# More difference steps in the early blocks, and an earlier pair of sums in block 22

## The chip, the cores and the metric

The kernel runs on one core of a Trainium2 chip. The metric is device time in microseconds for one execution. The kernel before takes 592.43 us in the median of three runs (592.17 to 593.26). "PE" is the matrix engine TensorE, "PEld" its weight loads, "DVE" VectorE, "ACT" ScalarE, "POOL" GpSimd, and "SP" the engine that issues the stores.

## What is computed

The input x has 8 batches of 3008 rows and 256 columns. The reference takes the real part of the two-dimensional Fourier transform of each batch, multiplies the 24064 resulting rows by a 256 x 2048 matrix, takes the squared positive part, and multiplies by a 2048 x 256 matrix:

```python
X = np.fft.fft(x, axis=1)
X = np.fft.fft(X, axis=2)
x = X.real.reshape(B * S, D)
h = np.maximum(x @ w_in, 0.0)
return (h * h @ w_out).astype(np.float32)
```

## The kernel before

**Blocks and their two halves.** The output rows come in pairs: from the same cosine part and sine part of a transformed row (tiles `zc` and `zs`) follow the row k, as P+Q, and its mirror image, as P-Q. P is the product of the weights with `zc`, Q that with `zs`. So the kernel works on 12040 columns instead of 24064 rows. They are cut into 25 blocks (`wins`, w = 0 to 24); block 0 has 240 columns, block 1 has 512, blocks 2 and 3 have 376 each, block 4 has 512, block 5 has 448, the others 512 and the last one 360. Each block fills a tile `h2` of 16 chunks of the 2048 hidden features, with the P+Q results in half 0 (columns 0 to wn) and the P-Q results in half 1, and the block after it multiplies that `h2` by the second weight matrix (`ffn2_steps`, L713 to L757).

**Steps.** A block has eight steps s, two chunks of 128 features each. There are two kinds of steps (loop from L1054):

- A plain step: `pq` (L917) puts P+Q into a PSUM bank with four matmuls; ScalarE rectifies it into half 0 (`first`, `relu`, L966 and L946); `turn` (L941) adds -2Q with two more matmuls; ScalarE rectifies P-Q into half 1. The squares of both halves are done by VectorE as one operation (`power`, L958), which `keep` (L955) puts on a list that `settle` (L843) empties in the following step.
- A difference step, one of those listed in `diff`: `cosines` (L926) puts only P into the bank. VectorE computes t2 = -2P + N from it (`twice`, L932). Two matmuls add Q (`sines`, L936), and may do so only when `twice` has read the bank. ScalarE rectifies P+Q, and VectorE gets the other half as the saturated sum of t2 and the bank (the custom operation at L951). No `turn` is needed, so PE runs four matmuls and not six. N is the Nyquist row that the turned weights would have contributed; it comes in a tile `n2` per step. Half 0 is squared by ScalarE (`power_act`, L962, over the list `plus`), half 1 by VectorE, alone or with another step's.

**N rows.** `spread_nyq` (L851) stores one row of `zs` to DRAM from ScalarE's queue (`rd`) and loads it back to 128 partitions from GpSimd's queue (`zn`). `nyq_rows` (L858) then makes `n2` from it, two GpSimd operations per step; three such tiles exist. `nyq` (L984) calls them in the block before, from step `hi` on, and for what is left in step 0.

**Between the matmuls of a step** `others` (L971) issues what else is due: a share of the block before's second layer (a quarter of its 256 columns per job; jobs 0 to 7 are the groups 0 and 1 of 128 columns, then each group has four jobs, one per quarter of the 16 chunks), jobs of the transform (`at`), and, in steps `lo` to `hi` - 1, the matmuls that make `zc` and `zs` of the next block (`z_steps`, L538). Each of these two parts ends with a copy on ScalarE (L570) for the first columns and with `apart` (L585, VectorE L588) for the rest, called "the sums" here. If the next step is a difference step (`held["on"]`), the sums wait in `held["jobs"]` and are issued by `let_go` at the end of the next `settle`, so behind that step's `twice` and squares.

**Order.** All engines issue in the order in which the program names the instructions. The order is written by hand: `pend` holds the second rectifier of a difference step until after the next `twice` if the next step is a difference step too; `aside` holds squares until the next plain step, where they go behind its `pq`; `aside_act` holds squares for ScalarE, issued by `act_squares` at the end of a step. In blocks 3 and 4 the squares of step 6 go as one through `aside` (`twin`). Blocks 21, 23 and 24, and block 22 from step 6 on, have a third PSUM bank for steps (`px`).

**Where difference steps stand before.** Blocks 0 to 2 have none; blocks 3, 4 and 5 have steps 4 and 6; block 22 has 1, 2, 4, 5, 6, 7 and block 23 has 1, 2, 3, 5, 6, 7.

Of the kernel before, what the change touches and what calls it, by code (L numbers as in the profile page):

```python
# [29 lines left out]
def kernel(  # L30
# [49 lines left out]
    NW = len(wins)  # L80
# [687 lines left out]
    NST = NFC // 2  # L768
# [3 lines left out]
    diff[NW - 4] = diff[NW - 2] = (1, 2, 3, 5, 6, 7)  # L772
    diff[NW - 1] = (1, 2, 3, 4, 5, 6, 7)
    diff[NW - 3] = (1, 2, 4, 5, 6, 7)
    threes = (NW - 4, NW - 2, NW - 1)
    pairs = []
    by_act = (2, 5)
# [3 lines left out]
    def put(w, s, i, name, *k, d=at_of):  # L781
        d[w][s].append(lambda: folds[i][name](*k))
# [7 lines left out]
    for i in range(2, B):  # L790
        b0 = (win_of(col_of[i, 0]) + win_of(col_of[i - 1, 1])) // 2 - 1
        tight = b0 - 2 in [(win_of(col_of[j, 0]) + win_of(col_of[j - 1, 1])) // 2 - 1 for j in range(2, i)]
        near = i == 2 or tight
        at_of[b0 - 1][0].append(lambda i=i: make(i))
        calm = not near and not need[b0]
        at_of[b0 - 2][5 if calm else 7].append(lambda i=i: load_rows(i))
        backs.append(b0)
        late(b0 + 1, 3, i, 0)
        late(b0 + 1, 4, i, 1)
        for k in (2, 3, 4):  # L800
            late(b0 + 1, 5, i, k)
        put(b0 - 1, 4 if tight else 3 if i == 2 else 5 if near else 1 if calm else 3, i, "d_rows")
        put(b0 - 1, 5 if near else 3, i, "d_even", 0)
        put(b0 - 1, (6 if tight else 7) if near else 5, i, "d_even", 1)
        put(b0 if i == 2 else b0 - 1, 0 if i == 2 else 7, i, "n_cos")
        put(b0, 0, i, "d_odd", 0)
        put(b0, 1, i, "d_odd", 1)
        put(b0, 2, i, "n_sin")
        put(b0, 3, i, "even")
        put(b0, 4, i, "away")  # L810
        put(b0, 5, i, "odds")
        put(b0, 6, i, "back")
        put(b0, 6, i, "nyq", d=post_of)
        if i + 1 < B and (win_of(col_of[i + 1, 0]) + win_of(col_of[i, 1])) // 2 - 1 > b0 + 2:
            put(b0 + 1, 2, i, "load")
        else:
            put(b0, 7, i, "load")
        if b0 > 5:
            diff[b0] = (2, 4, 6, 7) if tight else (2, 4, 6)
            diff[b0 + 1] = (1, 2, 4, 6, 7)  # L820
            shared.append(b0 + 1)
        if calm:
            diff[b0 - 1] = (1, 2, 4, 6, 7)
            shared.append(b0 - 1)
            pairs.append(b0 - 1)
        if tight:
            diff[b0 - 1] = (1, 2, 4)
            shared.remove(b0 - 1)
# [5 lines left out]
    third = []  # L834
    aside = []
    aside_act = []

    def act_squares():
        run(*aside_act)
# [3 lines left out]
    def settle():  # L843
        for k in kept:
            k()
        kept.clear()
        let_go()
# [19 lines left out]
    for w in range(NW):  # L867
# [16 lines left out]
        if w == 1:  # L884
            fj = fold_jobs(1)
            at = [[], fj[0:1], fj[1:2], fj[2:3], fj[3:5], [], [], []]
            post[5] = fj[5:6]
        elif w == 2:
            te = table_steps(1)
            at = [[folds[1]["even"], folds[1]["away"]], [lambda: te["freq"](), lambda: te["args"](0)], [lambda: f0s["v_part"](0)], [lambda: f0s["v_part"](1), f0s["even"], f0s["away"], f0s["back"]],  # L890
                  [lambda: te["turns"](0)], [lambda: te["mods"](0)], [lambda: te["absm"](0), lambda: te["sins"](0)], [lambda: te["coss"](0)]]
        elif w == 3:
            at[0] = [lambda: te["weigh"]()]
            for st in range(5):
                at[1 + st // 3] = at[1 + st // 3] + f0s["late"][st : st + 1]
            at[3] = [folds[1]["back"]]
            lo, hi = 3, NST - 1
        elif w == win_of(col_of[1, 1]) - 1:
            for st in range(5):
                at[min(st, 3)] += folds[1]["late"][st : st + 1]  # L900
            lo, hi = 4, NST - 1
# [53 lines left out]
        def keep(*k):  # L955
            kept.append(lambda p=power: p(*k))
# [61 lines left out]
        if w == 0:  # L1018
            run(lambda: quad(0), lambda: quad_relu(0, 0), lambda: quad(1), lambda: quad_relu(1, 0))
            run(lambda: gh_step(2, False), lambda: gh_turn(2))  # L1020
            run(lambda: quad_turn(0), lambda: quad_relu(0, 1), lambda: quad_turn(1), lambda: quad_relu(1, 1))
            run(lambda: gh_step(3, False), lambda: gh_turn(3))
            run(lambda: quad(2), lambda: quad_relu(2, 0), lambda: quad(3), lambda: quad_relu(3, 0), *rm[1::2])
            run(lambda: quad_turn(2), lambda: quad_relu(2, 1), lambda: quad_turn(3), lambda: quad_relu(3, 1), *(lambda p=p: quad_power(p) for p in range(4)))
        elif w == 1:
            zl = [j for zu, part, h in zj for j in zu(part, h)]
            for p in range(NST // 2):
                s0, s1 = 2 * p, 2 * p + 1
                f2q = spread(f2, p, NST // 2)
                n = len(f2q) // 4  # L1030
                pq(s0)
                if p < 2:
                    settle()
                relu(s0, 0)
                pq(s1)
                relu(s1, 0)
                if s1 == NST - 1:
                    run(*post[s0 - 1])
                    settle()
                    power(s1, 0, 1)  # L1040
                    run(*zl)
                run(*f2q[0:n])
                turn(s0)
                run(*f2q[n : 2 * n])
                turn(s1)
                relu(s0, 1)
                relu(s1, 1)
                run(*at[s0], *at[s1], *f2q[2 * n :])
                if p == 2:
                    kept.pop(0)()  # L1050
                keep(s0, 0, 2)
                keep(s1, int(s1 == NST - 1), 2)
            gh_nyq()
        for s in range(NST) if w > 1 else ():  # L1054
            held["on"] = s + 1 in diff.get(w, ())
            if w == NW - 3 and s == 6:
                more_banks()
            if s in diff.get(w, ()):
                cosines(s)
                twice(s)  # L1060
                if w in pairs and s == 4:
                    kept.extend(aside)
                    aside.clear()
                run(*pend)
                pend.clear()
                settle()
                if made[s + 1]:
                    run(*plus)
                    plus.clear()
                others(s)  # L1070
                sines(s)
                first(s)
                twin = w < 5 and s == 6
                whole = twin or w in shared and s == 4 or w in threes[:2] or w in pairs or w == NW - 3 or w == NW - 1 and s in by_act
                pend.append(lambda s=s, r=relu, k=keep, whole=whole: (r(s, 1), whole or k(s, 1, 2)))
                if w in threes[:2] and s % 4 == 1 or w in pairs and s in (1, 6) or w == NW - 3 and s in (1, 4):
                    aside.append(lambda s=s, p=power: p(s, 1, 2, 2))
                if not made[s + 3]:
                    run(*pend)
                    pend.clear()  # L1080
                if twin:
                    aside.append(lambda s=s, p=power: p(s, 0, 2))
                else:
                    plus.append(lambda s=s, p=power_act: p(s))
                act_squares()
                if w == NW - 3 and s == 6:
                    aside.append(lambda s=s, p=power: p(s, 1, 2))
                if w in threes[:2] and s % 4 == 3 or w == NW - 3 and s == 7 or w == NW - 1 and s in by_act:
                    aside_act.append(lambda s=s, p=power_act: p(s, 1))
                nyq(s)  # L1090
                continue
            if made[s] and made[s + 1] and w not in threes and w not in pairs:
                f2s[s].pop(0)()
            pq(s)
            if not (w in pairs and s == 3):
                kept.extend(aside)
                aside.clear()
            settle()
            first(s)
            if s == NST - 1:  # L1100
                power(s, 0, 1)
            others(s)
            nyq(s)
            turn(s)
            relu(s, 1)
            act_squares()
            if w in shared and s == 5:
                power_act(4, 1)
            keep(s, int(s == NST - 1), 2)
        settle()  # L1110
        old = (w, h2)
    run(*plus)
# [33 lines left out]
```

## Time and profile before

| what | value |
|---|---|
| median of 3 runs | 592.43 us (592.17 to 593.26) |
| the profiled execution | 592.23 us |
| its span | 590.5 us |
| granted TensorE clock, mean | 0.999 |
| blocks 2 and 3 | 48.36 to 69.97 and 69.97 to 88.63 us |
| block 5 | 110.18 to 132.53 us |
| blocks 22 and 23 | 510.02 to 534.16 and 534.16 to 556.43 us |

The span is the time between the first and the last profiled instruction; 1.7 us of the execution lie around it. A row of a timeline reads: start, duration, engine, line of the kernel, operation, what it writes and from what, shape, count, and in square brackets how long the engine stood idle before it and what ended that. Consecutive instructions of one kind are one row. The starts of matmuls are as recorded, their ends are modelled and lie in the next matmul, so durations of matmuls are read from start to start.

### The profile page before, as it was taken

To read this page: it belongs to the slowest core of one execution; us is meant where nothing else is said; L and a number is where in the kernel's file an instruction comes from. 1 tells how busy PE (TensorE), PEld (TensorE's weight loads), DVE (VectorE), ACT (ScalarE), POOL (GpSimd) and SP (SyncE) were. 2 spreads that over 40 slices of the span, in tenths; PEclk is the share of its full clock that TensorE was granted. 3 is DMA by queue.
4 is the path that set the end of the run, shared out by engine and by line. 5 is a ranking of instruction groups with operands and counts; after the bars stand their busy time and mean duration, and the time that the engine had idled before them with its cause. 6 is when DMAs were issued, how large, how long until landed. Compare 5 with 4: busy or idle time off the path is not lost. (4 is left out here: it accounts for less than half of the span.)

```text
span 590.5 us, 11333 instructions
## 1 busy us (share of the span) xinstructions
PE 580.8 (98%) x4408; PEld 424.2 (72%) x4408; DVE 503.5 (85%) x579; ACT 474.2 (80%) x630; POOL 266.2 (45%) x325
## 2 busy tenths in 40 slices
PE   8999999999999999999999999999999999999997
PEld 4567786776777777767777777777777777776786
DVE  7988687987889787988999799979899798888881
ACT  7796878867887787788888798878888788988982
POOL 8520423267324626382454651555605825437230
PEclk9999999999999999999999999999999999999999
DMA  8945421133612561237124441146312311211222
GB/s 150 179 88 128 125 73 44 55 101 72 136 48 55 132 137 55 70 92 163 42 58 118 93 116 52 39 122 122 84 40 89 99 48 41 60 47 47 61 57 71
DMA packets 37625, 50.33 MB, mean 85 GB/s; under 512 B 4589, under 2 KB 30755, under 8 KB 37571
## 3 DMA queue, kind: packets, MB, share of 16 engines
q0 software_dynamic: 10400, 24.94, 21.0%
q1 hardware_dynamic: 26899, 24.44, 13.7%
q8 instruction: 34, 0.56, 0.4%
q10 hardware_dynamic: 272, 0.23, 0.1%
q14 instruction: 20, 0.16, 0.1%
HBM read 36.42 MB, written 27.86 MB: 109 GB/s over the span
## 5 line engine op out<-in xcount | busy, mean ns | idle before, releaser
L730 PE MATMUL po<-wout,h 128*128 128x256 f16 (+1 forms) x3024 | 364.4, 273 | 0.0
L730 PEld LDWEIGHTS <-h 128*128 128x128 f16 (+1 forms) x3024 | 296.8, 98 | 74.8
L953 ACT ACTIVATE h<-ph 128x1024 f16<-128x1024 f32 (+3 forms) x264 | 252.6, 989 | 58.1 <-PE ph L939 38.0
L864 POOL TENSOR_SCALAR n<-zn,g2n 128x512 f32<-128x512 f16 (+3 forms) x188 | 177.1, 956 | 79.9 <-DMA zn<-rd 56.9
L960 DVE TENSOR_TENSOR h<-h 128x2048 f16<-128x2048 f16 (+5 forms) x175 | 175.1, 1009 | 18.1 <-ACT h L953 15.4
L934 DVE SCALAR_TENSOR_TENSOR t<-ph,n 128x1024 f32<-128x1024 f32 (+3 forms) x84 | 100.3, 1194 | 30.7 <-PE ph L930 21.9
L964 ACT ACTIVATE h<-h 128x1024 f16<-128x1024 f16 (+3 forms) x107 | 110.3, 1033 | 1.5 <-DVE zs L588 0.4
L951 DVE CUSTOM_DVE_ANT_0 h<-t,ph 128x1024 f16<-128x1024 f32 x75 | 91.1, 1215 | 12.0 <-ACT h L953 11.5
L856 POOL DMA_DIRECT2D zn<-rd x22 | 12.8, 582 | 139.9 <-DMA rd<-zs 126.0
L745 ACT ACTIVATE osb<-po 128x512 f32<-128x512 f32 (+3 forms) x95 | 54.9, 582 | 24.4 <-PE po L730 19.8
L921 PE MATMUL ph<-zc,gh 128*128 128x512 f16 (+2 forms) x180 | 66.1, 368 | 0.4 <-ACT h L1012 0.3
L922 PE MATMUL ph<-zs,gh 128*128 128x512 f16 (+2 forms) x180 | 66.1, 368 | 0.0
L944 PE MATMUL ph<-zs,gh 128*128 128x512 f16 (+2 forms) x180 | 51.4, 367 | 0.0
L939 PE MATMUL ph<-zs,gh 128*128 128x512 f16 (+3 forms) x168 | 49.0, 373 | 1.6 <-DVE t L934 1.1
L930 PE MATMUL ph<-zc,gh 128*128 128x512 f16 (+3 forms) x168 | 49.0, 373 | 0.0
L930 PEld LDWEIGHTS <-gh 128*128 128x128 f16 x188 | 18.4, 98 | 21.0
L921 PEld LDWEIGHTS <-gh 128*128 128x128 f16 x196 | 19.1, 97 | 20.0 <-DVE h L951 0.7
L922 PEld LDWEIGHTS <-gh 128*128 128x128 f16 x196 | 19.1, 98 | 19.8 <-issue 0.7
L953 ACT ACTIVATE h<-px 128x1024 f16<-128x1024 f32 (+1 forms) x26 | 26.1, 1006 | 3.6 <-PE px L939 3.1
L939 PEld LDWEIGHTS <-gh 128*128 128x128 f16 x188 | 17.6, 98 | 6.3 <-issue 3.3
L564 ACT ACTIVATE es<-pz 128x376 f32<-128x376 f32 (+1 forms) x32 | 14.8, 484 | 8.2 <-PE pz L559 8.2
L448 POOL DMA_INDIRECT rb<-scr,idx_r x16 | 18.3, 1142 | 4.9 <-issue 4.6
(154 smaller groups left out, 428.8 us busy)
## 6 DMA issues: line engine op xcount, KB each, us to landing
out_dram<-osb SPq DMA_DIRECT2D x77, 128.0 KB
xo<-in_x_dram POOLq DMA_DIRECT2D x7, 768.0 KB, 7.0
scr<-ev POOLq DMA_DIRECT2D x8, 390.0 KB, 4.7
zn<-rd POOLq DMA_DIRECT2D x19, 128.0 KB, 4.3
rb<-scr POOLq DMA_DIRECT2D x16, 130.0 KB, 4.2
out_dram<-osb SPq DMA_DIRECT2D x12, 94.0 KB
w<-in_moe_w_in_dram POOLq DMA_DIRECT2D x2, 512.0 KB, 9.1
wout<-in_moe_w_out_dram POOLq DMA_DIRECT2D x1, 1024.0 KB
```

The source lines that it names most:

```text
L730: nc.tensor.matmul(po[0:m, j * D : (j + 1) * D], h2[:, fc, q : q + m], wout16[:, fc, :], start=(fc == 0 and not both), stop=(fc == NFC - 1 ...
L745: nc.scalar.activation(osb[0:mm].rearrange("p s d -> p (s d)")[:, lo:hi], po[0:mm, lo:hi], AF.Copy, bias=0.0, scale=HS * HS)
L864: nc.gpsimd.tensor_scalar(out=n2[:, a, 0:wn1], in0=zns[wt][:, 0:wn1], scalar1=g2n[:, fc : fc + 1], scalar2=1.0, op0=ALU.mult, op1=ALU.mult)
L921: nc.tensor.matmul(ph[:, a, 0:wn], gh[:, 0, f0 : f0 + P], zcw[:, 0:wn], start=True, stop=False)
L922: nc.tensor.matmul(ph[:, a, 0:wn], gh[:, 1, f0 : f0 + P], zsw[:, 0:wn], start=False, stop=True)
L930: nc.tensor.matmul(ph[:, a, 0:wn], gh[:, 0, f0 : f0 + P], zcw[:, 0:wn], start=True, stop=True)
L934: nc.vector.scalar_tensor_tensor(out=t2[:, :, 0:wn], in0=phs[s][:, :, 0:wn], scalar=-2.0, in1=n2s[w, s][:, :, 0:wn], op0=ALU.mult, op1=ALU ...
L939: nc.tensor.matmul(phs[s][:, a, 0:wn], gh[:, 1, f0 : f0 + P], zsw[:, 0:wn], start=False, stop=True, skip_group_check=True)
L951: nc.vector._custom_dve(TENSOR_ADD_SAT, out=h, in0=t2s[s][:, :, 0:wn], in1=phs[s][:, :, 0:wn], s0=BIG, s1=0.0)
L953: nc.scalar.activation(h, phs[s][:, :, 0:wn], AF.Relu, bias=0.0, scale=-1.0)
L960: nc.vector.tensor_tensor(h, h, h, op=ALU.mult)
L964: nc.scalar.activation(h, h, AF.Square, bias=0.0, scale=1.0)
```

## The change

- Block 2 gets two difference steps (4 and 6); its N row is sent at the start of the block. Blocks 3 and 5 get step 7 as a third.
- In block 3 the matmuls for block 4's columns are spread over steps 3 to 5 and no longer 3 to 6, and block 4's N row is sent a step earlier.
- The plain steps 0 to 3 of block 5 and step 3 of block 22 have half 1 squared by ScalarE (`halved`).
- `odds` of batch index 2 moves from step 5 to step 4 of block 5. `twin` stays with blocks 3 and 4.
- In step 4 of block 22 the held sums are issued ahead of the squares. The square of half 1 of step 6 goes to a new list `later`, which joins `aside` in step 1 of block 23, where before it joined `aside` at once.

```diff
+    diff[2] = (4, 6)
+    diff[3] = (4, 6, 7)
+    diff[5] = (4, 6, 7)
...
-        put(b0, 5, i, "odds")
+        put(b0, 4 if i == 2 else 5, i, "odds")
...
+    later = []
...
-            lo, hi = 3, NST - 1
+            lo, hi = 3, NST - 2
...
+        if w == 2:
+            spread_nyq(w)
...
                 run(*pend)
                 pend.clear()
+                if w == NW - 3 and s == 4:
+                    let_go()
                 settle()
...
-                twin = w < 5 and s == 6
+                twin = w in (3, 4) and s == 6
...
                 if w == NW - 3 and s == 6:
-                    aside.append(lambda s=s, p=power: p(s, 1, 2))
+                    later.append(lambda s=s, p=power: p(s, 1, 2))
+                if w == NW - 2 and s == 1:
+                    aside.extend(later)
...
-            keep(s, int(s == NST - 1), 2)
+            halved = w == 5 and s < 4 or w == NW - 3 and s == 3
+            if halved:
+                aside_act.append(lambda s=s, p=power_act: p(s, 1))
+            keep(s, int(s == NST - 1), 1 if halved else 2)
```

## The prediction, made before the run

> **What bounds the kernel now.** I read the page's busy table first, then the waits of PE, and then the timelines of single engines at every place where the change puts or takes something.
>
> ```profile
> span 590.5 us, 11333 instructions
> PE 580.8 (98%) x4408; PEld 424.2 (72%) x4408; DVE 503.5 (85%) x579; ACT 474.2 (80%) x630; POOL 266.2 (45%) x325
> ...
> PE ph L939 <- DVE t L934: 1.1, 1, 1.1
> ```
>
> PE is busy for 580.8 of 590.5 us, and its weight loads (PEld) run beside the matmuls. So the time is the sum of the matmuls plus the few places where PE stands still. The longest wait of the steady blocks is a "sines" matmul (L939) that waited 1.1 us for `twice` on VectorE (L934), which must have read the bank before the sines are added to it. Whatever removes a matmul shortens the run by its start-to-start time, and whatever makes PE wait lengthens it by the whole wait, for nothing behind it has slack to give it back. DVE, ACT and POOL matter only through such waits. That is how I go through the change: matmuls saved, waits saved, waits made. All times are in the frame of the profiled run before.
>
> **Part 1: the turns that go.** A step that becomes a difference step runs no `turn` (two matmuls, L944). The timelines of PE in blocks 2 and 5 give its price.
>
> ```profile
> 61.55 0.48 PE L944 MATMUL ph<-zs,gh 128*128 128x376 f16 x2
> 61.86 0.32 PE L921 MATMUL ph<-zc,gh 128*128 128x376 f16 x1
> ...
> 121.33 0.54 PE L944 MATMUL ph<-zs,gh 128*128 128x448 f16 x2
> 121.70 0.54 PE L930 MATMUL ph<-zc,gh 128*128 128x448 f16 x2
> ```
>
> The ends are modelled and overlap, so I take start to start: 61.86 - 61.55 = 0.31 us for two matmuls of 376 columns, and 121.70 - 121.33 = 0.37 us for two of 448. Steps 4 and 6 of block 2 and step 7 of block 3 save 3 x 0.31, step 7 of block 5 saves 0.37: **-1.30 us**. ScalarE loses one rectifier and gains one half square in each such step, operations of like size, so I call that even. VectorE gets `twice` and the saturating add and gives half a square back; what hides that in block 2 stands in part 5. In block 5 four half squares more leave VectorE, so that it gives away about as much as it gets, and `odds` comes into a step in which VectorE waits for a rectifier; I cost both at nothing.
>
> **Part 2: block 22, sums ahead of the square.** PE and VectorE at steps 4 and 5:
>
> ```profile
> 525.54 1.91 PE L730 MATMUL po<-wout,h 128*128 128x256 f16 x16
> 528.51 0.59 PE L939 MATMUL ph<-zs,gh 128*128 128x512 f16 x2 [1.06 <-DVE t L934]
> ...
> 524.81 1.47 DVE L960 TENSOR_TENSOR h<-h 128x2048 f16<-128x2048 f16 x1 [0.39 <-ACT h L953]
> 526.20 0.60 DVE L588 SCALAR_TENSOR_TENSOR zs<-es,pz 128x16 f16<-128x16 f32 x2
> 526.72 0.60 DVE L588 SCALAR_TENSOR_TENSOR zc<-es,pz 128x16 f16<-128x16 f32 x2
> 527.25 1.21 DVE L934 SCALAR_TENSOR_TENSOR t<-ph,n 128x1024 f32<-128x1024 f32 x1
> ```
>
> The sixteen matmuls of the second layer from 525.54 take 1.74 us (546.43 to 548.17, rows of part 3), so the sines were due at 527.28 and came at 528.51: 1.23 us lost. VectorE was free at 524.42, waited 0.39 for a rectifier, squared both halves, summed (526.20 to 527.25 = 1.05) and only then began `twice`. Now the sums start at 524.4 and need no rectifier; they end at 525.45; the square is of one half, half of 1.47; `twice` runs from about 526.15 to 527.35. The sines lose some 0.1 us: **-1.1 us**. The other half of that square is one more activation on ScalarE, ahead of the next block's row transfer; ScalarE had waited for the late sines too, so I take nothing for it. If that cover is too small, the N rows of block 23 come later, and its first `twice` with them.
>
> **Part 3: the square of step 6 of block 22, half one.** It leaves step 0 of block 23, where it stood right ahead of `twice`, and goes through `later` into `aside` at step 1. From there it is issued at the next step that is no difference step, which is step 4, behind the square of steps 1 and 2.
>
> ```profile
> 537.63 1.91 PE L730 MATMUL po<-wout,h 128*128 128x256 f16 x16
> 539.91 0.59 PE L939 MATMUL px<-zs,gh 128*128 128x512 f16 x2 [0.37 <-DVE t L934]
> ...
> 538.05 0.68 DVE L960 TENSOR_TENSOR h<-h 128x1024 f16<-128x1024 f16 x1
> 538.65 1.21 DVE L934 SCALAR_TENSOR_TENSOR t<-px,n 128x1024 f32<-128x1024 f32 x1
> ```
>
> Where it leaves: the sines were due at 537.63 + 1.74 = 539.37 and came at 539.91. Without the square `twice` begins at 538.05 and ends at 539.26, in time: **-0.5 us**.
>
> ```profile
> 546.43 1.91 PE L730 MATMUL po<-wout,h 128*128 128x256 f16 x16
> 548.17 0.59 PE L944 MATMUL px<-zs,gh 128*128 128x512 f16 x2
> ...
> 546.88 1.22 DVE L951 CUSTOM_DVE_ANT_0 h<-t,ph 128x1024 f16<-128x1024 f32 x1 [0.88 <-ACT h L953]
> 548.01 1.22 DVE L960 TENSOR_TENSOR h<-h 128x2048 f16<-128x2048 f16 x1
> ```
>
> Where it goes: step 4 of block 23 runs jobs 16 to 19 of the 32 of block 22's second layer, four quarters of group 4. Group 4 is the first 128 columns of half one, and its last quarter takes chunks 12 to 15, that is steps 6 and 7. So the thirteenth of the sixteen matmuls loads as its weights what this square writes. It is due at 546.43 + 12 x 0.109 (1.74 / 16) = 547.74. VectorE ends the add of step 3, squares from 548.01, can begin our square at 549.15 and ends it 0.68 later, at 549.83. With some 0.1 us to load weights and start, PE waits **+2.2 us**. The bounds: if the square could run at once behind the add (548.01 to 548.69), 1.0; below that nothing in the queue's order allows. `twice` of step 5, which the longer queue would delay, comes after the wait of PE and finds VectorE idle.
>
> **Part 4: block 3, step 7.** The sums for block 4 are now made one step earlier, and step 7 has a `twice` of its own behind them. Before: VectorE, then PE, then ScalarE.
>
> ```profile
> 84.72 0.94 DVE L934 SCALAR_TENSOR_TENSOR t<-ph,n 128x752 f32<-128x752 f32 x1 [0.42 <-PE ph L930]
> 85.58 0.93 DVE L960 TENSOR_TENSOR h<-h 128x1504 f16<-128x1504 f16 x1
> 86.52 0.61 DVE L588 SCALAR_TENSOR_TENSOR zs<-es,pz 128x135 f16<-128x135 f32 x2
> 87.04 0.60 DVE L588 SCALAR_TENSOR_TENSOR zc<-es,pz 128x135 f16<-128x135 f32 x2
> 87.58 0.94 DVE L951 CUSTOM_DVE_ANT_1 h<-t,ph 128x752 f16<-128x752 f32 x1
> ...
> 88.31 0.48 PE L944 MATMUL ph<-zs,gh 128*128 128x376 f16 x2
> ...
> 84.49 0.83 ACT L953 ACTIVATE h<-ph 128x752 f16<-128x752 f32 x1
> 85.99 0.49 ACT L570 ACTIVATE zs<-pz 128x377 f16<-128x377 f32 x1 [0.67 <-PE pz L559]
> 86.38 0.48 ACT L570 ACTIVATE zc<-pz 128x377 f16<-128x377 f32 x1
> ```
>
> The sines of step 7 are due where its turn stood, less the two matmuls that no longer lie ahead: 88.31 - 0.31 = 88.00. On VectorE stand `twice` of step 6, the square of step 5, the four sums (held back to this place, since step 6 is a difference step) and then `twice` of step 7. Even in the places of before, 87.58 + 0.94 = 88.52 is 0.5 too late. But the square of step 5 waits for its second rectifier (84.49 to 85.32), and the two copies zs and zc (0.39 each, start to start) now come out of step 5, ahead of that rectifier: it ends at about 86.1. Square to 87.0, sums to 88.1, `twice` to 89.0: PE waits 1.05. The add of step 6 then frees its bank at about 89.9, where the first matmul of block 4 wants it, behind four matmuls that are pulled ahead: another 0.1. **+1.15 us**, bounds 0.5 and 1.3. Elsewhere in block 3 nothing holds PE.
>
> **Part 5: N rows in block 2.** A row goes out on ScalarE's queue at the start of the block (`rd`), comes back over POOL's queue on 128 partitions (`zn`), and POOL makes two tiles per step from it. The views of ScalarE, POOL, VectorE and of the tile zn:
>
> ```profile
> 48.24 0.65 ACT L745 ACTIVATE osb<-po 128x256 f32<-128x256 f32 x2
> 88.52 0.22 ACTq L855 DMA_DIRECT2D rd<-zs  x1
> 500.47 0.21 ACTq L855 DMA_DIRECT2D rd<-zs  x1
> ...
> 89.88 0.57 POOL L856 DMA_DIRECT2D zn<-rd  x1 [9.97 <-DMA rd<-zs]
> 505.18 0.62 POOL L856 DMA_DIRECT2D zn<-rd  x1 [5.27 <-DMA rd<-zs]
> 70.93 2.52 POOL L864 TENSOR_SCALAR n<-zn,g2n 128x376 f32<-128x376 f16 x4 [2.67 <-DMA zn<-rd]
> 114.74 7.71 POOL L864 TENSOR_SCALAR n<-zn,g2n 128x448 f32<-128x448 f16 x4 [2.80 <-DMA zn<-rd]
> ...
> 59.34 0.57 DVE L339 TENSOR_TENSOR ev<-w 128x768 f16<-128x768 f16 x1
> 65.88 0.94 DVE L960 TENSOR_TENSOR h<-h 128x1504 f16<-128x1504 f16 x1 [1.00 <-ACT h L953]
> ...
> DMA to landing us min/median/max: 3.2/4.0/5.8
> ```
>
> `rd` goes out at 48.9 and takes 1.4 (88.52 to 89.88) to 4.7 us (500.47 to 505.18), `zn` 3.2 to 5.8, the first two tiles 2 x 0.63. In the middle that is 48.9 + 3.0 + 4.0 + 1.3 = 57.2. `twice` of step 4 can begin at 59.9, when VectorE's fold ends, and must by 60.3 (sines due at 61.55 - 0.31 = 61.24, 0.94 for `twice`). So 3 us of cover. Behind the wait for `rd` on POOL stand the transfer of ev and, behind the tiles, its small memsets; a fold of VectorE waits for that transfer's end, and I take it to be in time. `twice` and the add, 0.94 us each (84.72, 87.58), less half of the 0.93 of a whole square (85.58), are 1.4 us more per difference step on VectorE; it had idle time of about 1 us in a step (65.88), and the non-difference step between takes the rest. I take 0.1 us.
>
> **The sum.** -1.30 - 1.1 - 0.5 + 2.2 + 1.15 + 0.1 = +0.55, say +0.5 us. The profiled execution took 592.23 us (span 590.5 and 1.7 around it), the median of three runs is 592.43: 592.7 and 592.9. I predict **592.9 us**, own range 592.0 to 593.7. A measurement of this kernel can tell about 0.2% (1.2 us) from no change, so this is "the same".
>
> **Rivals.** (a) The moved square doesn't hold PE. For it: one place loses 0.5 us by this very square, and the aim of a later place is plain. Against it: the weights of the thirteenth matmul are its output, and VectorE's queue is in order. Time: 592.9 - 2.2 = 590.7. (b) The sums of block 3 don't hold PE, because they come out of the queue before the square or the rectifier is earlier than I think: 592.9 - 1.2 = 591.7, the same still. (a) and (b) together: 589.5. (c) The slower side: the N rows of block 2 come late. With both transfers at their longest the row is there at 48.9 + 4.7 + 5.8 = 59.4. POOL's four tiles took 2.52 us at 70.93 but 7.71 us at 114.74, beside folds and squares on VectorE, 1.9 each; with that price the first pair is ready at 63.3, `twice` ends at 64.2, PE waits 3.0 us: 595.9. It decides from 60.3 on; from 61 on the run is slower than can be told from no change.
>
> The Trainium skill, "SBUF — State Buffer", section "Who interferes with whom", speaks against adding work to POOL here: a VectorE instruction with two inputs in SBUF contends with a GpSimd instruction that reads SBUF. The trace agrees, with 1.9 against 0.6 us for a tile. By that rule the tiles of block 2, which meet folds of VectorE that last until 59.9, go by the long price; that alone (row at 55.9, pair at 59.8) still leaves them in time.
>
> **Chances.** Forecast 0.48 (of it 0.05 over the upper bound), (a) 0.15, (b) 0.12 (of it 0.01 under the lower bound), both 0.04, (c), at half its price or more, 0.21. Faster by over 0.2%: 0.15 + 0.04 + 0.01 = 0.20. Slower: 0.21 + 0.05 = 0.26. Within: 0.54. The range for 8 in 10 leaves out the case of both and the longer part of (c), and takes in (a): 590.5 to 594.4.
>
> **What would show it.** Right: 8 `turn` matmuls fewer; no wait of over 0.2 us at the sines of block 22, step 5, and block 23, step 1; a new wait of about 2 us inside the sixteen second-layer matmuls of block 23, step 4, ended by a square (L960); a new wait of about 1 us at the sines of block 3, step 7, ended by `twice`. Wrong: second-layer matmuls in step 4 without a gap; a wait at the sines of block 2, step 4, ended by `twice` that itself waited for POOL; or a time under 591.2 or over 593.6.

## The result, and the profile after

The changed kernel takes **595.93 us** in the median of six runs (595.26 to 596.53), the kernel before 592.48 us beside it (591.95 to 593.26): ratio 1.0058, interval 1.0048 to 1.0069, so 3.45 us more. The forecast was 592.9 us with a range up to 594.4; the time lies above it, on the side that had a chance of 0.26. It is, by coincidence, the 595.9 us that rival (c) gave; the cause that (c) named didn't occur, as shown below. The profiled execution took 596.53 us, the longest of the six.

The head of the page, and behind it the waits of PE (for whom, us in total, times, the longest):

```profile
span 594.8 us, 11341 instructions
...
PE 581.0 (98%) x4400; PEld 423.1 (71%) x4400; DVE 507.9 (85%) x585; ACT 478.6 (80%) x635; POOL 269.7 (45%) x334
```

```profile
PE po L730 <- DVE h L964: 2.0, 1, 2.0
...
PE ph L943 <- DVE t L938: 1.2, 3, 0.9
PE ph L948 <- ACT h L957: 0.8, 3, 0.3
```

The line numbers of the steps are four higher than before. PE runs eight matmuls fewer, four turns of two, and in return the three kinds of wait shown here stand in the list, of which before's had only the second. The first two were forecast. The third, `turn` (L948) waiting for a rectifier (L957), was not.

**The moved square** (block 23, step 4). PE and VectorE in after:

```profile
547.55 1.47 PE L730 MATMUL po<-wout,h 128*128 128x256 f16 x12
551.01 0.61 PE L730 MATMUL po<-wout,h 128*128 128x256 f16 x4 [1.99 <-DVE h L964]
...
548.00 1.22 DVE L955 CUSTOM_DVE_ANT_0 h<-t,ph 128x1024 f16<-128x1024 f32 x1 [0.88 <-ACT h L957]
549.14 1.82 DVE L964 TENSOR_TENSOR h<-h 128x2048 f16<-128x2048 f16 x2
```

The sixteen second-layer matmuls are cut into twelve and four, at the thirteenth as the prediction had it. Due at 547.55 + 12 x 1.74 / 16 = 548.85, it came at 551.01: 2.16 us. On VectorE two squares stand behind the add; the second is the moved one.

**Block 3, step 7.** VectorE and PE in after:

```profile
85.17 0.94 DVE L938 SCALAR_TENSOR_TENSOR t<-ph,n 128x752 f32<-128x752 f32 x1 [0.69 <-PE ph L934]
86.30 0.94 DVE L964 TENSOR_TENSOR h<-h 128x1504 f16<-128x1504 f16 x1 [0.18 <-ACT h L957]
...
88.19 0.94 DVE L938 SCALAR_TENSOR_TENSOR t<-ph,n 128x752 f32<-128x752 f32 x1
...
89.18 0.48 PE L943 MATMUL ph<-zs,gh 128*128 128x376 f16 x2 [0.86 <-DVE t L938]
```

The square waits for its rectifier, the sums follow, `twice` begins at 88.19 and the sines lose 1.03 us from start to start. This, too, is the forecast chain.

**Block 5, plain steps: what was missed.** First ScalarE, then PE in after:

```profile
117.61 0.91 ACT L957 ACTIVATE h<-ph 128x896 f16<-128x896 f32 x1
118.41 0.95 ACT L968 ACTIVATE h<-h 128x896 f16<-128x896 f16 x1
119.25 0.92 ACT L957 ACTIVATE h<-ph 128x896 f16<-128x896 f32 x1
...
118.06 1.91 PE L730 MATMUL po<-wout,h 128*128 128x256 f16 x16
120.22 0.54 PE L948 MATMUL ph<-zs,gh 128*128 128x448 f16 x2 [0.26 <-ACT h L957]
```

The turn adds -2Q to the bank that holds P+Q, so it may start only when the rectifier of P+Q has read that bank. That rectifier (119.25, of step 2) stands behind the half square of step 0 (118.41), which `act_squares` issues at the end of step 1. Its bank was ready at 118.06; the turn was due after sixteen matmuls, at 118.06 + 1.74 = 119.80, and came at 120.22. The like place of before, one step later, has no square between the two rectifiers of neighbouring steps:

```profile
119.02 1.73 ACT L953 ACTIVATE h<-ph 128x896 f16<-128x896 f32 x2 [1.05 <-PE ph L944]
```

Its second rectifier ends at 120.75, and the turn that waits for it starts at 121.33: 0.58 us to spare, less than the 0.84 that a half square takes (118.41 to 119.25). The turns at 123.41 (step 3) and 129.10 (step 5) of after lose 0.31 us each in the same way: 1.04 us in block 5. Two more turns wait for the same reason elsewhere. ScalarE and PE in after, around the start of block 3:

```profile
68.53 0.83 ACT L968 ACTIVATE h<-h 128x752 f16<-128x752 f16 x1
69.25 0.92 ACT L274 ACTIVATE cos<-t,halfpi 128x754 f16<-128x754 f32 x1
70.07 0.59 ACT L745 ACTIVATE osb<-po 128x512 f32<-128x512 f32 x1
70.55 1.49 ACT L957 ACTIVATE h<-ph 128x752 f16<-128x752 f32 x2
...
70.30 1.47 PE L730 MATMUL po<-wout,h 128*128 128x256 f16 x12
72.09 0.48 PE L948 MATMUL ph<-zs,gh 128*128 128x376 f16 x2 [0.31 <-ACT h L957]
```

Block 2's step 6 is a difference step now, so half 0 of it is squared on ScalarE (68.53), ahead of a table of cosines, a copy and two rectifiers; the turn comes 0.48 us after the twelve matmuls. At the start of block 4, PE and ScalarE:

```profile
90.91 1.04 PE L730 MATMUL po<-wout,h 128*128 128x256 f16 x8
92.18 0.59 PE L948 MATMUL ph<-zs,gh 128*128 128x512 f16 x2 [0.24 <-ACT h L957]
...
91.11 1.02 ACT L957 ACTIVATE h<-ph 128x1024 f16<-128x1024 f32 x1 [0.61 <-PE ph L926]
```

Step 7 of block 3 being a difference step, one second-layer job is pulled ahead of the bank's first matmuls, and only eight matmuls (0.87 us), no longer twelve, lie between the bank and its turn, while the rectifier takes 1.02: the turn, due at 91.78, loses 0.40 us. Together the turns lose 0.48 + 0.40 + 1.04 = **1.92 us** that no part of the prediction contains.

**The end.** The last store's issue on ScalarE's queue, in before and in after:

```profile
586.68 0.33 ACTq L709 DMA_DIRECT2D out_dram<-osb  x1
```

```profile
589.97 0.33 ACTq L709 DMA_DIRECT2D out_dram<-osb  x1
```

From that issue to the end of the span pass 590.5 - 586.7 = 3.8 us before and 594.8 - 590.0 = 4.8 after. The matmuls end 3.29 us later, the span 4.3.

**The N rows of block 2** were in time. GpSimd in after:

```profile
50.53 0.60 POOL L860 DMA_DIRECT2D zn<-rd  x1 [7.10 <-DMA rd<-zs]
...
53.86 3.89 POOL L868 TENSOR_SCALAR n<-zn,g2n 128x376 f32<-128x376 f16 x4 [1.34 <-DMA zn<-rd]
```

The pair for step 4 is there by about 55.8, `twice` needs it at 59.9. Rival (c) fell.

### The profile page after: what moved, and what is told of

It reads as the page before. It is cut to its first block, busy times and chain, and to the rows that moved or that the text cites. A ratio compares the mean times of both kernels' runs of the same rounds, so it can differ in the third digit from the quotient of the medians.

```text
span 594.8 us, 11341 instructions
## 1 busy us (share of the span) xinstructions
PE 581.0 (98%) x4400; PEld 423.1 (71%) x4400; DVE 507.9 (85%) x585; ACT 478.6 (80%) x635; POOL 269.7 (45%) x334
## 4 chain that ended last, share of the span: by engine, by line
PE 74%; DVE 9%; ACT 7%; DMA 4%; issue 4%; POOL 1%; SPq 0%; ACTq 0%; POOLq 0%; DVEq 0%
PE po L730 42%; PE ph L943 5%; PE ph L948 5%; PE ph L934 5%; PE ph L925 5%; PE ph L926 5%; ACT h L957 3%; PE pz L559 3%; DVE h L964 3%; DVE t L938 3%; DVE h L955 2%; DMA out_dram<-osb 1%; DMA xo<-in_x_dram,idx_r 1%; ACT h L968 1%; DMA zn<-rd 1%
## 5 line engine op out<-in xcount | busy, mean ns | idle before, releaser
L957 ACT ACTIVATE h<-ph 128x1024 f16<-128x1024 f32 (+3 forms) x260 | 250.2, 991 | 57.2 <-PE ph L943 36.0
L868 POOL TENSOR_SCALAR n<-zn,g2n 128x512 f32<-128x512 f16 (+3 forms) x196 | 180.4, 934 | 86.9 <-DMA zn<-rd 53.6
L964 DVE TENSOR_TENSOR h<-h 128x2048 f16<-128x2048 f16 (+5 forms) x173 | 171.5, 999 | 11.8 <-ACT h L957 8.9
L938 DVE SCALAR_TENSOR_TENSOR t<-ph,n 128x1024 f32<-128x1024 f32 (+3 forms) x88 | 104.2, 1184 | 35.2 <-PE ph L934 27.2
L968 ACT ACTIVATE h<-h 128x1024 f16<-128x1024 f16 (+3 forms) x116 | 118.5, 1024 | 1.1
L925 PE MATMUL ph<-zc,gh 128*128 128x512 f16 (+3 forms) x172 | 63.5, 370 | 0.3 <-ACT h L1016 0.3
L926 PE MATMUL ph<-zs,gh 128*128 128x512 f16 (+3 forms) x172 | 63.5, 369 | 0.0
L943 PE MATMUL ph<-zs,gh 128*128 128x512 f16 (+3 forms) x176 | 50.9, 371 | 1.8 <-DVE t L938 1.2
L934 PE MATMUL ph<-zc,gh 128*128 128x512 f16 (+3 forms) x176 | 51.0, 371 | 0.0
L948 PE MATMUL ph<-zs,gh 128*128 128x512 f16 (+3 forms) x172 | 49.5, 369 | 1.1 <-ACT h L957 0.8
L934 PEld LDWEIGHTS <-gh 128*128 128x128 f16 x196 | 19.1, 98 | 21.6
L925 PEld LDWEIGHTS <-gh 128*128 128x128 f16 x188 | 18.3, 97 | 19.5 <-DVE h L955 0.7
L926 PEld LDWEIGHTS <-gh 128*128 128x128 f16 x188 | 18.4, 98 | 19.1 <-issue 0.7
L957 ACT ACTIVATE h<-px 128x1024 f16<-128x1024 f32 (+1 forms) x26 | 26.1, 1006 | 5.2 <-PE px L943 2.3
L943 PEld LDWEIGHTS <-gh 128*128 128x128 f16 x196 | 18.5, 98 | 6.5 <-issue 3.4
L948 PEld LDWEIGHTS <-gh 128*128 128x128 f16 x188 | 17.3, 97 | 5.0 <-issue 2.0
```

Source lines behind the costliest of these rows:

```text
L868: nc.gpsimd.tensor_scalar(out=n2[:, a, 0:wn1], in0=zns[wt][:, 0:wn1], scalar1=g2n[:, fc : fc + 1], scalar2=1.0, op0=ALU.mult, op1=ALU.mult)
L925: nc.tensor.matmul(ph[:, a, 0:wn], gh[:, 0, f0 : f0 + P], zcw[:, 0:wn], start=True, stop=False)
L926: nc.tensor.matmul(ph[:, a, 0:wn], gh[:, 1, f0 : f0 + P], zsw[:, 0:wn], start=False, stop=True)
L934: nc.tensor.matmul(ph[:, a, 0:wn], gh[:, 0, f0 : f0 + P], zcw[:, 0:wn], start=True, stop=True)
L938: nc.vector.scalar_tensor_tensor(out=t2[:, :, 0:wn], in0=phs[s][:, :, 0:wn], scalar=-2.0, in1=n2s[w, s][:, :, 0:wn], op0=ALU.mult, op1=ALU ...
L943: nc.tensor.matmul(phs[s][:, a, 0:wn], gh[:, 1, f0 : f0 + P], zsw[:, 0:wn], start=False, stop=True, skip_group_check=True)
```

## The experiments

Three theories. **A**: the time is the sum of the matmuls and PE's waits, and each wait belongs to one edit. **B**: the queues of VectorE and ScalarE are full, so a wait that is taken away returns elsewhere. **C**: a wait of 2 us on PE also lowers the granted clock behind it. A fourth, D, about the end of the program, came with the last run. The table holds each kernel's median less that of before beside it, and what its one profiled execution shows of it: PE's waits (every start-to-start time beyond a matmul's usual one, from 14 us on, added up; 7.75 us in before; matmuls that ran at a lowered clock count here too), the turns saved, and the time from the end of the last copy (L734), at which the last store goes out, to the end of the span (3.80 us in before), all as differences to before.

| kernel | measured | PE's waits | turns | end | sum |
|---|---|---|---|---|---|
| after | +3.45 | +4.34 | -1.30 | +1.01 | +4.05 |
| e1: moved square in step 3 | +1.55 | +1.80 | -1.30 | +0.99 | +1.49 |
| e3: block 3 with two steps | +2.50 | +2.45 | -0.99 | +1.02 | +2.48 |
| e4: block 22 alone | -0.56 | -0.77 | 0 | +0.36 | -0.41 |
| e5: e1, twin in block 2 | +0.62 | +1.13 | -1.30 | +1.02 | +0.85 |
| e6: e1, sums first in block 3 | +0.07 | +0.64 | -1.30 | +0.99 | +0.33 |
| e7: e1, no half squares in block 5 | -0.14 | +1.00 | -1.30 | +0.75 | +0.45 |
| e8: longer wait | +8.67 | +9.18 | -1.30 | +0.97 | +8.85 |
| e9: the cures together | -1.02 | -1.11 | -1.30 | +0.83 | -1.58 |
| e10: e9, block 4 shifted | -1.06 | -0.47 | -1.30 | +0.81 | -0.96 |
| e11: early blocks alone | +3.09 | +3.05 | -1.30 | +0.96 | +2.71 |
| e12: block 2's transfers alone | +0.92 | -0.04 | 0 | +0.82 | +0.78 |

Every sum is within 0.6 us of what was measured, most within 0.3. The sum is bookkeeping of one execution, with its first 14 us left out, set against a median of several; it checks that no large term is missing, and what tests theory A is whether a wait goes with its edit. e2 isn't in the table: its profiled execution, the longest of five, holds a drop of the clock, and by the same working its sum would be about +5 where +3.30 were measured.

**e1: the moved square one step earlier, behind step 3's `twice`.**

```diff
-                if w == NW - 2 and s == 1:
-                    aside.extend(later)
+                if w == NW - 2 and s == 2:
+                    kept.extend(later)
```

> The changed kernel (595.9 us) with one edit: the moved square of block 22 is issued in step 3 of block 23, where VectorE idled 0.88 us, and no longer in step 4. Theory A (the time is the matmuls plus PE's waits, and each wait belongs to one edit): the wait of 2.16 us inside the second layer of block 23, step 4, goes and nothing comes for it: 593.7 us, 2.2 less than the changed kernel. Rival B (the queues of VectorE and ScalarE are so full that a wait undone turns up at the next place): over half of it comes back at the sines of steps 3 or 5, 594.8 us or more.

593.71 us against 592.16 (ratio 1.0028, 1.0018 to 1.0038). PE in e1, at the place of the wait:

```profile
546.91 1.91 PE L730 MATMUL po<-wout,h 128*128 128x256 f16 x16
548.66 0.59 PE L948 MATMUL px<-zs,gh 128*128 128x512 f16 x2
```

The sixteen matmuls run through. The wait of 2.16 us is gone and none came in its place: A.

**e2: in block 5 the half square goes behind the next rectifier of P+Q instead of ahead of it.**

```diff
             first(s)
+            if w == 5:
+                act_squares()
```

> The changed kernel with one edit: in the plain steps of block 5 ScalarE does the half square of the step before right behind the first rectifier, and no longer behind the second one. Same instructions, another order on ScalarE alone. Theory A, with the step that the prediction lacked (the turn has to wait until the first rectifier has read the bank, and the half squares stand ahead of that rectifier): the three waits of the turn in block 5 (0.42, 0.31 and 0.31 us) go, 594.9 us. Rival B (the half squares are too much work for ScalarE in block 5 wherever they stand): the waits move to the second rectifier and the next step, 595.9 us.

595.46 us (ratio 1.0053, 1.0040 to 1.0066), between the 594.9 of A and the 595.9 of the rival. The waits of the turns of steps 2 and 3 are gone, so it was the order on ScalarE that made them. The third stayed: that square, step 3's, is issued at the end of step 4, a difference step, where the edit changes nothing. The median fell less than the two waits, which isn't explained; the profiled execution (596.37 us) for its part ran into a drop of the clock behind the 2 us wait. PE by windows around that wait, in e2 (length of the window, PE's busy time and matmuls, granted clock, share and rate of the DMA engines):

```profile
545.00:549.20 4.20, 2.23 (x17) 1.00 0.24 83
549.20:553.50 4.30, 4.28 (x20) 0.60 0.16 28
553.50:557.50 4.00, 4.00 (x31) 1.00 0.19 66
```

Finer windows show 1.00 until 550.03 and 0.50 from there to 553.44: the 0.60 is the mean of a stretch at full clock and 3.4 us at half. After's own profile shows no drop at that place. That is C, but not every time.

**e3: block 3 with two difference steps, as before.**

```diff
-    diff[3] = (4, 6, 7)
...
-            lo, hi = 3, NST - 2
+            lo, hi = 3, NST - 1
```

> The changed kernel with block 3 as before: difference steps 4 and 6 alone, the column matmuls over steps 3 to 6, block 4's row in step 7. Theory A: two turn matmuls come back (+0.31), the wait of the sines in step 7 (1.03), of the first matmul of block 4 (0.10) and of the turn in step 0 of block 4 (0.40) go: 594.7 us. Rival B: the early PE only meets VectorE's queue a step later, 595.5 us or more.

594.66 us (ratio 1.0054, 1.0038 to 1.0070; one of its six executions took 597.00). The waits of 1.03, 0.10 and, at the start of block 4, 0.40 us left together: all three belong to step 7 of block 3 and the earlier column matmuls that go with it, which save a turn of 0.31. A.

**e4: the kernel before with only block 22's part** (sums ahead of the square, its half square on ScalarE); the square of step 6 stays where it was.

```diff
+                if w == NW - 3 and s == 4:
+                    let_go()
...
+            halved = w == NW - 3 and s == 3
```

> The kernel before (592.5 us) with two edits: the sums of block 22, step 4, ahead of the squares, and half 1 of step 3 squared by ScalarE. Blocks 2 to 5 and the square of step 6 are as before. Theory A: the wait of 1.23 us at the sines of step 5 shrinks to 0.3, as in the changed kernel: 591.6 us. Rival B (the time saved is taken back by the late N rows of block 23 or by the 0.54 us wait in step 1 there, which grows): 592.5 us.

591.60 us (ratio 0.9991, 0.9983 to 1.0000). The change's part in block 22 seems a gain by itself, if a small one (the interval reaches 1). The square of step 6, left where it was, costs PE 0.66 us there (0.54 in before); moved, it cost 2.16.

**e5: e1, and block 2's squares of step 6 on VectorE as one.**

```diff
-                twin = w in (3, 4) and s == 6
+                twin = w < 5 and s == 6
```

> The kernel with the square in step 3 (593.7 us) and one edit: block 2 squares step 6 whole on VectorE (as blocks 3 and 4 do), so that ScalarE has one half square less ahead of the rectifiers at the start of block 3. Theory A (the turn waits for a first rectifier that other work of ScalarE holds up): the wait of 0.48 us at the turn of block 3, step 0, goes: 593.2 us. Rival B (VectorE takes on what ScalarE loses): a wait of the same size elsewhere in block 3, 593.7 us.

592.92 us (ratio 1.0010, 1.0001 to 1.0019). The turn of block 3, step 0, no longer waits: it was block 2's square on ScalarE.

**e6: e1, and in block 3 the sums and `twice` of step 7 go ahead of the square of step 5.**

```diff
-                settle()
+                if w == 3 and s == 6:
+                    let_go()
+                else:
+                    settle()
```

> The kernel with the square in step 3 (593.7 us) and one edit: in step 6 of block 3 the sums are issued without the square of step 5, which comes behind the next twice. Same instructions, another order on VectorE. Theory A (that square, waiting for a rectifier, and the sums stand ahead of the twice of step 7): the wait of 1.03 us there goes, and the turn of block 4, step 0, keeps its wait of 0.4: 592.7 us. Rival B (VectorE has too much work there in any order): the first matmul of block 4 waits instead, 593.4 us or more.

592.37 us (ratio 1.0001, 0.9992 to 1.0010). The waits of 1.03 and 0.10 us are gone; the turn of block 4, step 0, keeps its 0.40. So the square that waits for its rectifier was what held the sums, and `twice` with them.

**e7: e1, without the half squares on ScalarE in block 5.**

```diff
-            halved = w == 5 and s < 4 or w == NW - 3 and s == 3
+            halved = w == NW - 3 and s == 3
```

> The kernel with the square in step 3 (593.7 us) and one edit: block 5 leaves its squares to VectorE, whole, as before; step 7 there stays a difference step. Theory A: the three waits of the turn (1.04 us) go, and VectorE, which stood idle for 2.46 us ahead of the first twice of block 5, has room: 592.7 us. Rival B (the half squares on ScalarE were needed): the sines of steps 4, 6 or 7 wait for twice, 593.4 us or more.

592.16 us (ratio 1.0002, 0.9993 to 1.0011). PE at the same step of block 5 as above (the turn at 120.22 in after), in e7:

```profile
117.38 1.91 PE L730 MATMUL po<-wout,h 128*128 128x256 f16 x16
119.12 0.54 PE L948 MATMUL ph<-zs,gh 128*128 128x448 f16 x2
```

119.12 - 117.38 = 1.74: the turn is in time, and so are the others of the block. VectorE, which has the whole squares again, makes nobody wait.

**e8: after, with dead work on VectorE ahead of the squares of block 23, step 4**, so that PE's wait there gets longer.

```diff
+            if w == NW - 2 and s == 4:
+                pad = tmp.tile([P, 3, NE], F32, name="pad", tag="tm")
+                nc.vector.memset(pad, 0.0)
+                kept.insert(0, lambda: nc.vector.tensor_tensor(pad, pad, pad, op=ALU.mult))
```

> The changed kernel (595.9 us) with dead work on VectorE, about 1.9 us (a memset and a product of a scratch tile), ahead of the squares in step 4 of block 23, so that the wait of PE there, 2.16 us, becomes about 4. Theory A (waits and matmuls alone): 597.8 us. Theory C (a wait of PE of 2 us can lower its granted clock for the microseconds behind it, as one profile showed, 0.60 over 4.3 us, and a longer one does so each time): 599 us or more, with a stretch of granted clock well under 1 behind the wait.

600.97 us (ratio 1.0146, 1.0131 to 1.0162). The wait grew by 2.55 us, to 4.71, more than was meant. PE in e8, then the windows around it:

```profile
552.40 1.04 PE L730 MATMUL po<-wout,h 128*128 128x256 f16 x4 [4.55 <-DVE h L964]
...
554.93 3.04 PE L730 MATMUL po<-wout,h 128*128 128x256 f16 x16
```

```profile
548.00:553.00 5.00, 0.60 (x3) 0.74 0.14 29
553.00:558.00 5.00, 5.00 (x24) 0.58 0.02 3
558.00:563.00 5.00, 5.00 (x40) 1.00 0.16 52
```

In finer windows the granted clock is 0.50 from 550.40, within the wait, until about 557.2, so the matmuls behind the wait run at half the clock for 4.8 us; the stretch of 552.40 to 557.81 takes 5.41 us where 3.04 are usual. The wait costs 2.4 us more than its own length.

**e9, e10, e11.** e9 is e1 with the edits of e5, e6 and e7, as they stand above. e10 gives step 0 of block 4 its four matmuls back:

```diff
+        if w == 4:
+            for q in range(5):
+                f2s[q].append(f2s[q + 1].pop(0))
```

> e1 (moved square in step 3 of block 23) with the three single cures together: the square of step 6 of block 2 on VectorE, block 3's square of step 5 behind the sums of step 7, no half squares on ScalarE in block 5. Theory A: the waits are separate terms, so they add: 593.71 - 0.48 - 0.25 (block 3 step 0, block 23 step 1) - 1.13 (block 3 step 7, block 4 step 0's first wait) - 1.04 (three turns of block 5) = 590.8 us; what each cure gave by itself (0.79, 1.34, 1.55) adds up to 590.0. One wait of 0.40 us stays, at the turn of step 0 of block 4. Theory B (the queues of ScalarE and VectorE are full, work put back on VectorE turns up as a wait elsewhere): 591.6 or more, with new waits of PE for VectorE in blocks 3 to 6.

591.07 us (590.31 to 591.32) against 592.09 (ratio 0.9980, 0.9971 to 0.9989): 0.2% faster than before, with an interval clear of 1, and faster than after. That is near A's 590.8. The only one of PE's new waits that is left in the early blocks, in the list of e9 (idle time; from start to start it is the 0.40 us of block 4, step 0):

```profile
PE ph L948 <- ACT h L957: 0.2, 1, 0.2
```

The waits nearly add up: in the table the cures take 0.67, 1.16 and 0.80 us off e1's when each stands alone, 2.63 in all, and 2.91 together. The times don't: measured beside before, the cures alone gave 0.93, 1.48 and 1.69 us, 4.10 in all, and together 2.57. Each alone gave more than the wait that it removes, and no run shows why.

> e9, and in block 4 each of the steps 1 to 5 gives its first second-layer part to the step before it, so that step 0 has 12 matmuls of the second layer between its sums and its turn again. If the wait of 0.40 us there is lack of cover for the rectifier: it goes, 0.4 us below e9, about 590.4 us by theory A's waits. If it is ScalarE that comes late whatever stands ahead of it on PE: no change against e9. Rival: step 5, which has one part fewer now, waits by as much, and the time is e9's.

591.03 us (ratio 0.9979, 0.9970 to 0.9988), e9's time. The turn of step 0 doesn't wait (90.38), so its wait was lack of cover. But PE in e10 waits at another place:

```profile
90.38 0.59 PE L951 MATMUL ph<-zs,gh 128*128 128x512 f16 x2
...
106.54 0.59 PE L946 MATMUL ph<-zs,gh 128*128 128x512 f16 x2 [0.36 <-DVE t L941]
```

There, late in the same block, PE loses 0.53 us where e9 loses 0.09. At step 5 itself it loses 0.10. The rival held, mostly at a later step than the one it named: block 4 has no spare cover to lend, which is B in small. Why step 6 pays, no run isolates.

e11 is after without what the change does in blocks 22 and 23:

```diff
-                if w == NW - 3 and s == 4:
-                    let_go()
...
-                    later.append(lambda s=s, p=power: p(s, 1, 2))
-                if w == NW - 2 and s == 1:
-                    aside.extend(later)
+                    aside.append(lambda s=s, p=power: p(s, 1, 2))
...
-            halved = w == 5 and s < 4 or w == NW - 3 and s == 3
+            halved = w == 5 and s < 4
```

> The change in blocks 2, 3 and 5 alone; blocks 22 and 23 as before. Theory A: matmuls -1.30 us, PE's waits +0.48 +1.03 +0.10 +0.40 +1.04 = +3.05 us in blocks 3 to 5: 592.5 + 1.75 = 594.2 us, and with the 0.33 us that the start of block 1 came later in the profiled run 594.6 us; by the runs so far (e1 593.71 less what block 22 alone gave, 0.6 to 0.9) 594.3 to 594.6. Theory B (the early blocks catch up on later slack): within 0.5 us of before.

595.18 us (ratio 1.0051, 1.0037 to 1.0065), about 0.6 to 1 us above what PE's waits alone had made expected. All waits of the early blocks are there as in after, none is caught up later. What was over is of the size of the end's column, and that led to e12.

**e12: the kernel before with block 2's row transfers, out and back, and nobody to read them.**

```diff
+        if w == 2:
+            spread_nyq(w)
```

> The kernel before, with nothing of the change but the two transfers that fetch the Nyquist row of block 2 (out and back); nobody reads what they bring. It leaves PE's work as it is. Open point: PE's matmuls and waits account for all but about 0.8 us of after's loss; in the profiled runs the time from the issue of the last store to the end of the span was 3.8 us before (and 4.1 with block 22 alone) and 4.6 to 4.8 in all ten kernels with the early steps. Theory D (the two more transfers shift which of the program's transfers the end of the program waits for last, and what it still goes through behind it): 592.1 + 0.4 to 0.9 = 592.5 to 593.0 us, with 4.2 us or more from the last store's issue to the end, and PE's waits as before. If the tail is chance, or goes with something else of the change: 592.1 us, 3.8 to 4.1 us at the end. Rival: the transfer on ScalarE's queue holds ScalarE and PE waits in block 2: a new wait there, with the tail as before.

593.16 us (592.63 to 593.85) against 592.24 (ratio 1.0014, 1.0005 to 1.0023). PE's waits are those of before. The head of e12's page, and then its last store:

```profile
span 591.4 us, 11336 instructions
```

```profile
586.82 0.33 ACTq L709 DMA_DIRECT2D out_dram<-osb  x1
```

591.4 - 586.8 = 4.6 us at the end instead of 3.8. Two transfers some 540 us earlier make the program end later after its last store: that much is shown. The semaphore records of the traces show where. The stores and the outgoing row transfers (`rd`) take eight semaphores in turn, 336 uses in before and 337 in e12, and at the end SP waits for the eight in a fixed order, about 0.06 us each when they are already set. In before the last store has the eighth; SP passes it at 589.56 and is done. In e12 the last store has the first; SP passes it at 590.07 and goes through the other seven until 590.51. All twelve kernels with these transfers end like e12 in this, and before and e4 alike with the eighth. That one transfer more thus costs 0.44 us of the 0.82. The other 0.38 is that the last store landed 3.27 us after the last copy instead of 2.89; in e4, without any added transfer, it was 3.25, so that part need not come from the transfers.

## Why the prediction was wrong

Its sum was +0.5 us; 3.45 us were measured. What failed is the step that put ScalarE's part at nothing; the waits it did list came. By its own steps:

- **Part 1, the turns**: -1.30 forecast, and as much is missing from PE's matmuls. Right. **Wrong in the same part: the sentence that calls ScalarE's exchange of a rectifier for a half square even, and block 5's half squares and `odds` nothing.** ScalarE's busy time rose by 4.4 us (478.6 against 474.2), which by itself would have held up nothing; the order did. The half square stands ahead of the rectifier of a later step, and that one releases a bank to `turn`. It cost 1.04 us in block 5 (e7, e2) and 0.48 in block 3, step 0 (e5). The prediction had counted what VectorE holds up on PE and left out what ScalarE holds up there, though its own statement of the bound says that DVE, ACT and POOL matter "only through such waits".
- **Part 2, the sums ahead of the square**: -1.1 forecast, -0.91 seen (1.23 to 0.32). The half square behind the sums was the mis-sized term. VectorE and PE in after:

```profile
527.71 1.03 DVE L964 TENSOR_TENSOR h<-h 128x1024 f16<-128x1024 f16 x1
528.67 1.21 DVE L938 SCALAR_TENSOR_TENSOR t<-ph,n 128x1024 f32<-128x1024 f32 x1
...
527.87 1.91 PE L730 MATMUL po<-wout,h 128*128 128x256 f16 x16
529.93 0.59 PE L943 MATMUL ph<-zs,gh 128*128 128x512 f16 x2 [0.15 <-DVE t L938]
```

  It took 0.96 us from start to start, where half of 1.47 was assumed. The sines, due at 527.87 + 1.74 = 529.61, lost 0.32, more than the 0.2 that the prediction's own list of signs allowed.
- **Part 3, the moved square**: +2.2 forecast, +2.16 seen, gone in e1. Right, and with it rival (a) fell. Where the square left, -0.5 forecast and -0.30 seen (0.54 to 0.24): with it gone, `twice` waited for its N row instead, which the prediction had named in part 2 as the thing that comes late if cover is too small. That differs from execution to execution: of the ten profiled kernels with this edit four lose 0.24 to 0.32 us there and six at most 0.06, as forecast. VectorE and PE in after:

```profile
539.76 1.22 DVE L938 SCALAR_TENSOR_TENSOR t<-px,n 128x1024 f32<-128x1024 f32 x1 [0.51 <-POOL n L868]
...
539.06 1.91 PE L730 MATMUL po<-wout,h 128*128 128x256 f16 x16
541.04 0.59 PE L943 MATMUL px<-zs,gh 128*128 128x512 f16 x2
```

- **Part 4, block 3, step 7**: +1.15 forecast, 1.03 + 0.10 seen; e6 shows the cause to be the one named. Right, and rival (b) fell. **Wrong: "Elsewhere in block 3 nothing holds PE."** Step 0 of block 3 lost 0.48 (e5). And where two difference steps precede a plain one, the kernel pulls a second-layer job ahead of `pq`: the prediction counts these four matmuls as cover for block 4's first matmul, and not that they are a third of the cover of its first turn: 0.40 (e3, e10).
- **Part 5, the N rows**: +0.1 forecast, nothing seen; the rows were early. But the two transfers that carry them came with a longer end, by about 0.8 us (e12: +0.92 in the time, of which 0.44 is traced to them above). The prediction has no term and no bound for it.

The bill: the prediction's terms at the sizes seen make -1.30 - 0.91 + 2.16 - 0.30 + 1.13 = +0.78, the turns +1.92, the end +0.92 by e12: 3.6 where 3.45 were measured. After's profile also has waits of 0.2 us more in blocks 7 and 8; in e2 and e3, with the same steps there, they aren't longer than in before, so they aren't put down to the change. All the new waits that the last part of the prediction listed came; the fault lies in what it didn't list. A search over every instruction that a moved ScalarE operation now stands ahead of would have found the turns: the half square's 0.84 us stand against the 0.58 that before has to spare there.

## What to carry to other kernels

Where PE accumulates into a bank that another engine has still to read, the reader's place in its queue is part of PE's critical path: an operation that is moved to an engine because it "has time" must go behind such readers, not ahead of them (e2, e7). Price each added step in every queue it enters, and count how many matmuls are left as cover between a bank's last write and the next one; a job pulled ahead at one end takes the cover from the other (e3, e10). In a kernel with PE at 98% the books of PE's waits, the matmuls saved and the end of the program closed to 0.6 us for twelve kernels (not for e2), so a part of a change that is worth 0.3 us is worth keeping only if it makes no wait.

## What the runs showed of the hardware

A wait of PE can cost more than its length. Behind 1.99 us of idle time the granted clock fell to 0.50 for 3.4 us in e2 (549.23 to 553.96 took 4.73 us where the same matmuls take 3.04) and stayed at 1.00 in after. In e8 it was 0.50 for 6.8 us, from 2.5 us into the wait of 4.55 us until 4.8 us behind it. The Trainium skill, "TensorE: Matmul & The Clock Gate", section "HAM oscillation — how this bites in real kernels", gives the rule that PE shouldn't stand idle for more than about 3.4 us. e8, with 4.55 us, agrees, though its clock fell after 2.5; e2 shows that at times 2 us are enough.

The start of the program differs from run to run. PE from 4 to 7 us, in before and in e2, whose program is the same there:

```profile
4.00:7.00 3.00, 3.00 (x13) 1.00 1.06 208
```

```profile
4.00:7.00 3.00, 3.00 (x20) 1.00 1.05 207
```

13 matmuls of 384 columns fall into these 3 us in the one and 20 in the other. From one start to the next they take 0.32 us at first and 0.16 later; the change comes at 6.0 us in before and at 3.8 in e2. The clock column reads 1.00 all the same. So PE begins at half its pace and changes over at a moment that the kernel alone doesn't set. Over the kernels profiled here the time that PE loses to this adds up to between 1.5 and 2.9 us, so one profiled execution should be compared with another place by place, not by its span.
